# Q and K of groups two to five through DRAM by chunk, in one fixed order

## The chip, the cores and the metric

The kernel runs on one core of a Trainium2 chip. The metric is the device time of one execution in microseconds (us): TensorE (PE), VectorE (DVE), ScalarE (ACT), GpSimd (POOL) and SyncE (SP), which here only issues transfers, work side by side, and the time ends with the last of them.

## The reference

Two layers follow each other. The first is a gated linear recurrence over 768 steps, for 4 batches and 8 heads of width 48, with a complex gate a:

```python
scale = np.minimum(mag, 0.999) / (mag + 1e-06)
for t in range(S):
    new_re = ar * S_re - ai * S_im
    new_im = ar * S_im + ai * S_re
    S_re, S_im = (new_re + np.einsum('bhd,bhe->bhde', k[:, :, t], v[:, :, t]), new_im)
    y[:, :, t] = np.einsum('bhd,bhde->bhe', q[:, :, t], S_re)
```

The second takes y as 3072 rows x of 384 numbers through four experts of width 1024, weighted by the row's normalised probabilities p:

```python
for e in range(E):
    h = np.maximum(x @ w1[e], 0.0)
    out += p[:, e:e + 1] * (h @ w2[e])
```

## The kernel before

The 3072 steps are cut into 12 groups of 256 (G), numbered 0 to 11, three to a batch, and each group into two chunks of 128 (C). The recurrence is turned into matmuls: `norm` and `prefix` build the running products A of the gate, `finish` makes from them Q (q times A, in `head`) and K (k times the inverse of A, in `tail`, lines 435 to 443: five DVE instructions for the whole group, or five for each chunk). Both have the channels on the partitions, in rows of 128 steps; the matmuls want them by head, with the real part in partitions 0 to 47 and the imaginary part in 64 to 111. That turn is made by a trip through DRAM (`trip`, lines 447 to 459): two stores of a tile (real, imaginary), `q_d<-Q` or `k_d<-K` at line 451, and two loads back, `Qst<-q_d` or `Kst<-k_d` at line 456. All go through SP's queue, which takes them in order, each with a wait for what it needs. There is one buffer each of K, Qst and Kst, so a trip back can't begin before the last use of the group before.

For each chunk the attention then takes on PE: `turned` (K turned by the identity into KT, `ktp` L487), `increment` (`dp` L505, the chunk's addition to the state), `scores` (`sc` L517, Kst against Qst), and `values` (`yp` L531 from the state, L536 from the scores). `attention` (lines 606 to 624) does this for groups from 2 on, in three pieces, and the second chunk's scores stand in the second piece.

The MoE's first two experts run in the same stretch: while the attention of group g is made ready, the block of group g - 1 goes through 8 pairs of weight tiles, twice over 12 x 256 steps in all, with `ph` (L179, x times w1), `hh` and `hl` (the two parts of the ReLU's result, L188 on ACT and L189 on DVE) and `po` (L198, times w2); each expert's result is stored in DRAM (`acc_d`, from POOL's queue). From about 555 us on the other two experts run over blocks of 512 rows (L817, L830).

Several things set the order of the work. `moe1` calls `between(k)` ahead of each pair of weight tiles. There `advance` takes steps from the generator `stream`, which holds the vector work of the groups ahead, by a budget of STEP = 3.4 us a call, counted by estimates that the generator yields; and pieces of the attention are taken at k = first, first + 1 and first + 2. A scheduler then orders the instructions of each engine by its own estimate, where no dependence and no `behind` (an order without a semaphore) sets it. So the same Python order can come out in another order on an engine. In `front` (lines 664 to 719) the groups of HALF = (2, 3) make K by chunk and send each chunk of K alone, while Q goes as a whole; from group 4 on both go as a whole.

Of the kernel before, what the change touches and what calls it, by code (L numbers as in the profile page):

```python
# [57 lines left out]
NSEL = 2  # L58
XSEL = 3
FIRST = {1: 5, 2: 5, 3: 4, 4: 3}  # L60
STEP = 3.4
MORE = (1.9, 1.9, 0.5)
HALF = (2, 3)
HOFF = 96
WIDE = 32 + P + 48
DMA_SCRATCH = 4096
# [2 lines left out]
def fast_path(ctx, tc, qkP, aP, vP, probsP, w, out, flag):  # L69
# [159 lines left out]
    with ExitStack() as c1:  # L229
# [160 lines left out]
        def finish(g, A, qk):  # L390
            s = tmp(f"s2{g}")
            u = tmp(f"u2{g}")
            Q = big.tile([P, 2, NR, C + 1], F32, tag="tmp", name=f"Q{g}", bufs=TMP)
            K = big.tile([P, 2, NR, C], F32, tag="K", name=f"K{g}", bufs=1)

            def im(ap):
                return ap.rearrange("p (i m) -> p i m", i=SEG)

            def some(ap, lo, hi):
                if hi - lo == CG:  # L400
                    return ap.rearrange("p i m -> p (i m)")
# [12 lines left out]

            def head(lo, hi):
                nc.scalar.activation(some(a2a, lo, hi), some(A[:, 0], lo, hi), AF.Square)
                nc.scalar.activation(some(b2a, lo, hi), some(A[:, 1], lo, hi), AF.Square)
                for c in range(lo, hi):
                    a2, ic = some(a2a, c, c + 1), some(i0a, c, c + 1)
                    red = nc.vector.tensor_tensor_reduce(a2, a2, some(b2a, c, c + 1), scale=1.0, scalar=3e38,  # L420
                                                         op0=ALU.add, op1=ALU.min, accum_out=st_a2[:, c, g:g + 1])
                    nc.scalar.activation(ic, a2, AF.Ln, scale=2.0 ** A2_LOG[c], bias=a2b)
                    last_act = nc.scalar.activation(ic, ic, AF.Exp, scale=-1.0, bias=a2e[:, c:c + 1])
                for c in range(2):
                    ins = nc.vector.tensor_tensor(dst(Q[:, c, :, :C], lo, hi), rows(A[:, c], lo, hi),
                                                  rows(qk[:, 0], lo, hi), op=ALU.mult)
                    if g < NSEL and lo == 1:
                        behind(ins, red)
                if hi == CG:
                    nc.scalar.activation(Q[:, :, :, C].rearrange("p c (j n) -> p c j n", n=CG),  # L430
                                         A[:, :, SEG - 1, NS - 1::NS].unsqueeze(3).broadcast_to([P, 2, NJ, CG]),
                                         AF.Copy)
                return last_act

            def tail(lo, hi):
                a2, i0, t, kn = (some(x, lo, hi) for x in (a2a, i0a, ta, qk[:, 1]))
                nc.vector.tensor_tensor(t, a2, i0, op=ALU.mult)
                nc.vector.scalar_tensor_tensor(t, t, 2.0, i0, op0=ALU.subtract, op1=ALU.mult)
                nc.vector.tensor_tensor(t, kn, t, op=ALU.mult)
                for c in range(2):  # L440
                    last_dve = nc.vector.tensor_tensor(dst(K[:, c], lo, hi), rows(A[:, c], lo, hi), rows(ta, lo, hi),  # L441
                                                       op=ALU.mult)
                return last_dve

            return Q, K, head, tail

        def trip(nm, X, dst, lo=0, hi=CG):
            w = X.shape[-1] if hi == CG else C
            dt = dram.tile([2, HD, hi - lo, w], F32, name=nm)
            for c in range(2):  # L450
                nc.sync.dma_start(dt[c].rearrange("(j p) n t -> p j n t", p=P),
                                  X[:, c].rearrange("p (j n) t -> p j n t", n=CG)[:, :, lo:hi, :w])

            def back():
                for c in range(2):
                    landed = nc.sync.dma_start(dst[c * IM:c * IM + D, :, lo:hi, :w],
                                               dt[c].rearrange("(h d) n t -> d h n t", d=D))
                return landed
            return back

        def t_factors(g):
# [10 lines left out]
        def chunk(g, c, K, y):  # L472
# [8 lines left out]
            def turned():  # L481
                if last and g >= NSEL:
                    return
                for i in range(2):
                    kt_ps = ps_a.tile([P, HD], F32, tag="pa", name=f"ktp{g}_{c}_{i}")
                    for j in range(NJ):
                        ins = nc.tensor.transpose(kt_ps[:, j * P:(j + 1) * P], K[:, i, j * CG + c, :], ident)  # L487
                    nc.scalar.activation(KT[:, :, i * IM:i * IM + D],
                                         kt_ps.rearrange("p (h d) -> p h d", d=D), AF.Copy)
                return ins  # L490
# [173 lines left out]
        def front(g, A, qk):  # L664
# [34 lines left out]
            yield 3.9  # L699
            last["act"] = head(0, CG)  # L700
            yield 3.0
            qb = trip(f"q_d{g}", Q, Qst)
            if g in HALF:
                kb = []
                for c in range(CG):
                    last["dve"] = tail(c, c + 1)
                    yield 2.7
                    kb.append(trip(f"k_d{g}_{c}", K, Kst, c, c + 1))
                    if c == 0:
                        qb()  # L710
                for back in kb:
                    last["q"] = back()
            else:
                last["dve"] = tail(0, CG)
                yield 4.8
                kb = trip(f"k_d{g}", K, Kst)
                qb()
                last["q"] = kb()
            todo[g] = attention(g, (Q, K))
# [31 lines left out]
                        yield g, r  # L751

        work = stream()
        spent = {"g": 1, "us": 0.0}

        def advance(us, upto):
            spent["us"] -= us
            while spent["us"] < 0 and spent["g"] <= upto:
                r = next(work, None)
                if r is None:  # L760
                    spent["g"] = NG
                    return
                spent["g"], cost = r
                spent["us"] += cost

        nk = NF1 // 2
        for g in range(1, NG + 1):
# [3 lines left out]
            end = first + len(MORE) - 1  # L771

            def between(k, g=g, first=first, end=end):
                advance(STEP + (MORE[k - first] if first <= k <= end else 0.0), g + 1)
                if g == 1:
                    for i in range(NPRE + 2 * k, min(NPRE + 2 * k + 2, NF1)):
                        add_w(i, wts["hh"] if k else wts["x"])
                if g < NG and first <= k <= end:
# [2 lines left out]
                    r = next(todo[g], None)  # L781
                    if r is not None:
                        x[g] = split_x(g, r) if g < NSEL else r
                if k == max(end, nk - 1) and g in x and g >= NSEL:
                    x[g] = split_x(g, x[g])

            moe1(g - 1, *x.pop(g - 1), between)
            for k in range(nk, end + 1):
# [269 lines left out]
```

## Time and profile before

| | |
|---|---|
| median of 3 runs | 1018.09 us (1017.57 to 1020.13) |
| the profiled execution | 1015.63 us, its span 1013.9 us |
| mean granted clock of PE | 0.991 |
| busy: PE, DVE, ACT, POOL | 982.5, 591.2, 363.4, 34.4 us |
| PE busy, 0 to 110 us | 89.9 us |
| PE busy, 110 to 280 us (MoE blocks of groups 1 to 5 in the main) | 165.3 us |
| PE busy, 280 to 555 us | 275.0 us |
| PE busy, 555 to 1014 us | 452.3 us |

A row of a timeline is the start, the duration, the engine, the line, what it writes and reads, the shapes and how many in a row; in brackets stands the idle time of the engine ahead of it and what ended that. A row of waits has the total, the number and the longest. A row of the chain has start and duration of a piece of the chain of work that ended last. A matmul of two float32 operands counts twice, so that a chunk's eight scores are sixteen records. A stretch has its length, each engine's busy time (with instructions), PE's granted clock, the DMA engines' share and their GB/s.

### The profile page before, as it was taken

To read this page: it belongs to the slowest core of one execution; us is meant where nothing else is said; L and a number is where in the kernel's file an instruction comes from. 1 tells how busy PE (TensorE), PEld (TensorE's weight loads), DVE (VectorE), ACT (ScalarE), POOL (GpSimd) and SP (SyncE) were. 2 spreads that over 40 slices of the span, in tenths; PEclk is the share of its full clock that TensorE was granted. 3 is DMA by queue.
4 is the path that set the end of the run, shared out by engine and by line. 5 is a ranking of instruction groups with operands and counts; after the bars stand their busy time and mean duration, and the time that the engine had idled before them with its cause. 6 is when DMAs were issued, how large, how long until landed. Compare 5 with 4: busy or idle time off the path is not lost.

```text
span 1013.9 us, 16212 instructions
## 1 busy us (share of the span) xinstructions
PE 982.5 (97%) x6624; PEld 924.4 (91%) x6624; DVE 591.2 (58%) x1219; ACT 363.4 (36%) x653; POOL 34.4 (3%) x64
## 2 busy tenths in 40 slices
PE   4799999999999999999999999999999999999997
PEld 2699999999999999999999999989999999999996
DVE  6798988989797989888842363232232222321221
ACT  7746526436263553636332343121111211211110
POOL 5020000000000000000000000000000000000000
PEclk9899999999999999999999999999999999999999
DMA  9474356474554837457171691021030010100001
GB/s 318 148 147 150 82 154 155 154 184 125 149 164 119 213 99 196 129 145 198 54 164 33 232 334 41 1 88 38 1 125 1 32 63 1 63 1 1 32 1 35
DMA packets 78932, 110.78 MB, mean 109 GB/s; under 512 B 5440, under 2 KB 63344, under 8 KB 78848
## 3 DMA queue, kind: packets, MB, share of 16 engines
q1 hardware_dynamic: 74560, 94.53, 32.6%
q0 software_dynamic: 4288, 15.13, 5.0%
q8 instruction: 54, 0.88, 0.4%
q14 instruction: 30, 0.25, 0.1%
HBM read 73.71 MB, written 35.92 MB: 108 GB/s over the span
## 4 chain that ended last, share of the span: by engine, by line
PE 87%; DVE 4%; DMA 3%; ACT 2%; issue 1%; SPq 0%; DVEq 0%; ACTq 0%
PE pob L830 20%; PE phb L817 20%; PE ph L179 18%; PE po L198 17%; PE sc L517 5%; PE dp L505 2%; PE yp L536 2%; PE yp L531 2%; DMA Kst<-k_d 2%; PE ktp L487 1%; PE xp L567 1%; DMA k_d<-K 1%; DVE K L441 1%; PE qp L385 0%; DVE hl L189 0%
## 5 line engine op out<-in xcount | busy, mean ns | idle before, releaser
L823 DVE SCALAR_TENSOR_TENSOR hlb<-phb,hhb 128x512 fp32r<-128x512 f32 x96 | 66.4, 691 | 270.6 <-ACT hhb L822 270.6
L822 ACT ACTIVATE hhb<-phb 128x512 fp32r<-128x512 f32 x96 | 57.4, 598 | 314.6 <-PE phb L817 299.2
L830 PE MATMUL pob<-wlo,hhb 128*128 128x384 f32 x384 | 129.2, 337 | 0.0
L198 PE MATMUL po<-whi,hh 128*128 128x384 f32 x384 | 129.0, 338 | 0.0
L830 PE MATMUL pob<-whi,hhb 128*128 128x384 f32 x384 | 128.9, 336 | 0.0
L198 PE MATMUL po<-wlo,hh 128*128 128x384 f32 x384 | 128.8, 335 | 0.0
L198 PE MATMUL po<-whi,hl 128*128 128x384 f32 x384 | 124.4, 338 | 0.2 <-DVE hl L189 0.2
L830 PE MATMUL pob<-whi,hlb 128*128 128x384 f32 x384 | 120.4, 336 | 0.0
L188 ACT ACTIVATE hh<-ph 128x512 fp32r<-128x512 f32 x96 | 57.2, 596 | 158.3 <-PE ph L179 158.0
L179 PE MATMUL ph<-xha,whi 128*128 128x256 f32 x576 | 104.9, 287 | 0.8 <-ACT xha L166 0.8
L179 PE MATMUL ph<-xha,wlo 128*128 128x256 f32 x576 | 101.3, 283 | 0.0
L179 PE MATMUL ph<-xla,whi 128*128 128x256 f32 x576 | 101.0, 283 | 0.0
L189 DVE SCALAR_TENSOR_TENSOR hl<-ph,hh 128x512 fp32r<-128x512 f32 x96 | 66.1, 688 | 53.5 <-ACT hh L188 53.0
L817 PE MATMUL phb<-xhb,whi 128*128 128x512 f32 x288 | 91.8, 392 | 0.0
L179 PEld LDWEIGHTS ph<-xha,whi 128*128 128x128 f32 x576 | 86.1, 190 | 1.8 <-ACT xha L166 1.0
L179 PEld LDWEIGHTS ph<-xha,wlo 128*128 128x128 f32 x576 | 82.8, 190 | 0.5 <-issue 0.5
L179 PEld LDWEIGHTS ph<-xla,whi 128*128 128x128 f32 x576 | 82.8, 191 | 0.0
L817 PE MATMUL phb<-xlb,whi 128*128 128x512 f32 x288 | 82.7, 392 | 0.0
L817 PE MATMUL phb<-xhb,wlo 128*128 128x512 f32 x288 | 82.3, 393 | 0.0
L830 PEld LDWEIGHTS pob<-whi,hhb 128*128 128x128 f32 x384 | 72.1, 188 | 3.7
L830 PEld LDWEIGHTS pob<-wlo,hhb 128*128 128x128 f32 x384 | 72.1, 188 | 3.3
L198 PEld LDWEIGHTS po<-whi,hh 128*128 128x128 f32 x384 | 72.5, 189 | 0.5 <-issue 0.3
(165 smaller groups left out, 1574.8 us busy)
## 6 DMA issues: line engine op xcount, KB each, us to landing
wst<-w SPq DMA_DIRECT2D x25, 384.0 KB, 6.4
qk<-qkP SPq DMA_DIRECT2D x24, 384.0 KB, 6.5
acc_d<-acc POOLq DMA_DIRECT2D x24, 384.0 KB, 4.4
prev<-acc_d SPq DMA_DIRECT2D x24, 384.0 KB, 4.9
A<-aP SPq DMA_DIRECT2D x22, 384.0 KB, 7.9
q_d<-Q SPq DMA_DIRECT2D x20, 387.0 KB, 3.6
Qst<-q_d SPq DMA_DIRECT2D x20, 387.0 KB, 5.2
k_d<-K SPq DMA_DIRECT2D x16, 384.0 KB, 3.4
```

The source lines that it names most:

```text
L179: ins = nc.tensor.matmul(ph[:, u, :], wt[:, j * P:(j + 1) * P], xt[:, j, :], start=(n == 0), stop=(n == 3 * NJ - 1))
L188: wts["hh"] = nc.scalar.activation(hh, ph, AF.Relu)
L189: nc.vector.scalar_tensor_tensor(hl, ph, 0.0, hh, op0=ALU.max, op1=ALU.subtract)
L198: nc.tensor.matmul(po[t], ht[:, u, t * P:(t + 1) * P], wt[:, HD:], start=(i % FE == 0 and n == 0), stop=(i % FE == FE - 1 and n == 2))
L505: nc.tensor.matmul(d_ps[:, h, :], KT[:, h, :], vc[:, h * D:(h + 1) * D], start=True, stop=True)
L517: nc.tensor.matmul(s_ps[:, h, :], Kc[:, hf * 4 + h, :], Qc[:, hf * 4 + h, :], start=True, stop=True)
L531: ins = nc.tensor.matmul(yo, st[:, o:o + n], Qc[:, o // D, :], start=True, stop=False)
L536: ins = nc.tensor.matmul(yo, vc[:, o:o + n], sc[h // 4][:, h % 4, :], start=first, stop=True)
L817: nc.tensor.matmul(ph, wt[:, j * P:(j + 1) * P], xt[:, j, :], start=(n == 0), stop=(n == 3 * NJ - 1))
L822: nc.scalar.activation(hh, ph, AF.Relu)
L823: nc.vector.scalar_tensor_tensor(hl, ph, 0.0, hh, op0=ALU.max, op1=ALU.subtract)
L830: ins = nc.tensor.matmul(po[t], ht[:, t * P:(t + 1) * P], wt[:, HD:], start=(i % FE == 0 and n == 0), stop=(i % FE == FE - 1 and n == 2))
```

## The change

- HALF now holds groups 2 to 5. There K is made and sent by chunk, and so is Q: each chunk of Q has its own DRAM tile, its own two stores and two loads.
- One order of issue is set in SP's queue with `behind`: the stores of both chunks of Q, the return of Q's first chunk, the stores of K's first and of K's second chunk, the return of K's first chunk, of Q's second, of K's second. Before, the scheduler placed these by its estimate.
- `front` yields None between head and tail. `advance` then holds the stream until the attention of the group before has been emitted (`over`). K's buffer is taken when the tail begins, not with Q's.
- `between` takes the piece of the attention first and advances the stream after it; before it was the other way round. STEP becomes an empty table that gives 3.4 for every group, as before.

From group 6 on the trips go as a whole, as before, though hold and later `advance` act there too. Groups 0 and 1 go another way (`near_attention`).

```diff
-STEP = 3.4
+STEP = {}
-HALF = (2, 3)
+HALF = (2, 3, 4, 5)
...
-            K = big.tile([P, 2, NR, C], F32, tag="K", name=f"K{g}", bufs=1)
+            K = []
...
             def tail(lo, hi):
+                if not K:
+                    K.append(big.tile([P, 2, NR, C], F32, tag="K", name=f"K{g}", bufs=1))
...
-        def trip(nm, X, dst, lo=0, hi=CG):
+        def trip(nm, X, dst, lo=0, hi=CG, prev=None):
...
-                nc.sync.dma_start(dt[c].rearrange("(j p) n t -> p j n t", p=P),
+                sent = nc.sync.dma_start(dt[c].rearrange("(j p) n t -> p j n t", p=P),
...
+                if prev is not None:
+                    behind(sent, prev)
...
-            qb = trip(f"q_d{g}", Q, Qst)
             if g in HALF:
+                qb = [trip(f"q_d{g}_{c}", Q, Qst, c, c + 1) for c in range(CG)]
+                yield None
+                landed = qb[0](qb[1].sent)
                 kb = []
                 for c in range(CG):
                     last["dve"] = tail(c, c + 1)
                     yield 2.7
-                    kb.append(trip(f"k_d{g}_{c}", K, Kst, c, c + 1))
-                    if c == 0:
-                        qb()
-                for back in kb:
-                    last["q"] = back()
+                    kb.append(trip(f"k_d{g}_{c}", K[0], Kst, c, c + 1, landed if c == 0 else kb[0].sent))
+                landed = kb[0](kb[1].sent)
+                landed = qb[1](landed)
+                last["q"] = kb[1](landed)
             else:
+                qb = trip(f"q_d{g}", Q, Qst)
+                yield None
...
+        spent = {"g": 1, "us": 0.0, "hold": 0}
+        over = {0}
...
             while spent["us"] < 0 and spent["g"] <= upto:
+                if spent["hold"] not in over:
+                    spent["us"] = 0.0
+                    return
...
-                spent["us"] += cost
+                if cost is None:
+                    spent["hold"] = spent["g"] - 1
+                else:
+                    spent["us"] += cost
...
-                advance(STEP + (MORE[k - first] if first <= k <= end else 0.0), g + 1)
...
+                    if k == end:
+                        over.add(g)
                 if k == max(end, nk - 1) and g in x and g >= NSEL:
                     x[g] = split_x(g, x[g])
+                advance(STEP.get(g, 3.4) + (MORE[k - first] if first <= k <= end else 0.0), g + 1)
```

More of the change, by code (lines that the diff above doesn't have):

```diff
@@ L440, in tail @@
                 for c in range(2):
-                    last_dve = nc.vector.tensor_tensor(dst(K[:, c], lo, hi), rows(A[:, c], lo, hi), rows(ta, lo, hi),
+                    last_dve = nc.vector.tensor_tensor(dst(K[0][:, c], lo, hi), rows(A[:, c], lo, hi), rows(ta, lo, hi),
                                                        op=ALU.mult)
@@ L450, in trip, with back @@
             for c in range(2):
-                nc.sync.dma_start(dt[c].rearrange("(j p) n t -> p j n t", p=P),
-                                  X[:, c].rearrange("p (j n) t -> p j n t", n=CG)[:, :, lo:hi, :w])
-            def back():
+                sent = nc.sync.dma_start(dt[c].rearrange("(j p) n t -> p j n t", p=P),
+                                         X[:, c].rearrange("p (j n) t -> p j n t", n=CG)[:, :, lo:hi, :w])
+                if prev is not None:
+                    behind(sent, prev)
+            def back(prev=None):
                 for c in range(2):
@@ L457, in back @@
                                                dt[c].rearrange("(h d) n t -> d h n t", d=D))
+                    if prev is not None:
+                        behind(landed, prev)
                 return landed
+            back.sent = sent
             return back
@@ L486, in turned @@
                     for j in range(NJ):
-                        ins = nc.tensor.transpose(kt_ps[:, j * P:(j + 1) * P], K[:, i, j * CG + c, :], ident)
+                        ins = nc.tensor.transpose(kt_ps[:, j * P:(j + 1) * P], K[0][:, i, j * CG + c, :], ident)
                     nc.scalar.activation(KT[:, :, i * IM:i * IM + D],
@@ L707, in front @@
                     yield 2.7
-                    kb.append(trip(f"k_d{g}_{c}", K, Kst, c, c + 1))
-                    if c == 0:
-                        qb()
-                for back in kb:
-                    last["q"] = back()
-            else:
+                    kb.append(trip(f"k_d{g}_{c}", K[0], Kst, c, c + 1, landed if c == 0 else kb[0].sent))
+                landed = kb[0](kb[1].sent)
+                landed = qb[1](landed)
+                last["q"] = kb[1](landed)
+            else:
+                qb = trip(f"q_d{g}", Q, Qst)
+                yield None
                 last["dve"] = tail(0, CG)
                 yield 4.8
-                kb = trip(f"k_d{g}", K, Kst)
+                kb = trip(f"k_d{g}", K[0], Kst)
                 qb()
@@ L753, in fast_path @@
         work = stream()
-        spent = {"g": 1, "us": 0.0}
+        spent = {"g": 1, "us": 0.0, "hold": 0}
+        over = {0}
         def advance(us, upto):
```

## The prediction

> **What bounds the kernel now.** I read the page first, then who waited for whom on PE, PE's timeline at the waits, the busy time of short stretches, the chain of waits, and the transfers.
>
> ```profile
> PE 982.5 (97%) x6624; PEld 924.4 (91%) x6624; DVE 591.2 (58%) x1219; ACT 363.4 (36%) x653; POOL 34.4 (3%) x64
> PE lp L147 <- DMA wst<-w: 9.6, 1, 9.6
> PE qp L385 <- DVE Q L425: 6.3, 1, 6.3
> PE sc L517 <- DMA Kst<-k_d: 3.8, 3, 1.8
> PE po L198 <- DVE hl L189: 0.2, 1, 0.2
> ```
>
> PE is busy for 982.5 of 1013.9 us, and the change takes no matmul away, so only PE's idle time, or matmuls that run slowly, can be won. Of the waits the first two lie in the start, which the change does not touch. The one it touches is the third: scores (sc) three times wait for K's way back from DRAM, 3.8 us in all. The other half of the loss shows where those waits end:
>
> ```profile
> 136.00 2.05 PE L517 MATMUL sc<-Qst,Kst 112*128 112x128 f32 x16 [1.03 <-DMA Kst<-k_d]
> 137.99 0.43 PE L531 MATMUL yp<-Qst,G 112*64 112x128 f32 x4
> ...
> 220.84 1.38 PE L517 MATMUL sc<-Qst,Kst 112*128 112x128 f32 x5 [1.84 <-DMA Kst<-k_d]
> ...
> 220.84 3.65 PE sc L517 x16
> ...
> 268.28 3.47 PE L517 MATMUL sc<-Qst,Kst 112*128 112x128 f32 x16 [0.93 <-DMA Kst<-k_d]
> 271.67 0.60 PE L531 MATMUL yp<-Qst,G 112*48 112x128 f32 x4
> ```
>
> The waits are those of groups 2, 4 and 5 (1.03, 1.84, 0.93 us). The same sixteen score records take 2.05 us after the first, but 3.65 and 3.47 us after the others (the row without a shape is the chain's). The granted clock says why:
>
> ```profile
> 132.12:135.54 3.42, 2.86 (x25) 2.73 (x23) 2.40 (x7) 0.00 (x0) 0.00 (x0) 1.00 0.83 213
> 217.45:220.87 3.42, 1.58 (x18) 1.48 (x16) 1.96 (x5) 0.60 (x1) 0.00 (x0) 1.00 1.10 204
> 265.25:268.66 3.41, 2.48 (x24) 2.35 (x23) 2.44 (x7) 0.00 (x0) 0.00 (x0) 1.00 1.07 253
> 220.80:224.60 3.80, 3.76 (x18) 3.79 (x19) 1.10 (x4) 0.00 (x0) 0.00 (x0) 0.55 0.82 316
> 268.00:272.00 4.00, 3.72 (x20) 3.42 (x20) 1.65 (x5) 0.00 (x0) 0.00 (x0) 0.58 0.69 267
> ```
>
> The second column is PE's busy time, the third from the end the clock. 0.55 over 3.8 us is about 3.4 us at half speed. The stretches before had PE busy for 1.58 and 2.48 of 3.4 us; the one with 2.86 (group 2) was not followed by half speed. So a wait of about a microsecond here also costs the slow matmuls behind it: 3.65 - 2.05 = 1.60 us in group 4; in group 5 3.47 - 2.05 = 1.42 and 0.60 - 0.43 = 0.17 for the next four, 1.59. Waits and slow stretches together are 3.80 + 3.19 = 7.0 us, the most that this change can win.
>
> **The change part by part.** The chain of waits shows the way that is to be shortened, in groups 4 and 5 (start, length). Behind it stand the half-size transfers of group 3, which goes by chunk already (two issues on SP's queue, then us from issue to landing), and the two sizes of K's products (mean ns behind the comma):
>
> ```profile
> 210.85 3.83 DMA k_d<-K
> ...
> 214.70 6.00 DMA Kst<-k_d
> ...
> 255.53 1.83 DVE K L441 x2
> ...
> 257.37 2.86 DMA k_d<-K
> ...
> 260.29 7.94 DMA Kst<-k_d
> 166.31 0.91 SPq L451 DMA_DIRECT2D k_d<-K  x2
> k_d<-K SPq DMA_DIRECT2D x4, 192.0 KB, 4.2
> 171.03 0.84 SPq L456 DMA_DIRECT2D Kst<-k_d  x2
> DMA to landing us min/median/max: 3.2/3.5/3.7
> L441 DVE TENSOR_TENSOR K<-A,u 128x384 f32<-128x384 f32 x8 | 4.1, 551 | 0.0
> L441 DVE TENSOR_TENSOR K<-A,u 128x768 f32<-128x768 f32 x4 | 3.6, 951 | 0.0
> ```
>
> *Products by chunk (groups 4, 5).* Five instructions of 951 ns become ten of 551 (other tail lines have the same two sizes), 0.75 us more DVE work a group. This is what DVE does in group 4, after (u holds the steps of the tail, K its product; hl is the MoE's, G the state, L338 the next group's norm):
>
> ```order
> L439 TENSOR_TENSOR u_2091<-s_2090,u_2091 128x24x16
> L564 TENSOR_TENSOR G_1_2264<-G_1_2264,TA 112x384
> L440 SCALAR_TENSOR_TENSOR u_2091<-u_2091 128x24x16
> L189 SCALAR_TENSOR_TENSOR hl_0_2412<-ph_0_2392,hh_0_2411 128x512
> L441 TENSOR_TENSOR u_2091<-qk_2084,u_2091 128x24x16
> L338 TENSOR_TENSOR u_2535<-s_2534,u_2535 128x768
> L443 TENSOR_TENSOR K_2441<-A_1594,u_2091 128x8x3x16 x2
> L189 SCALAR_TENSOR_TENSOR hl_1_2467<-ph_1_2447,hh_1_2466 128x512
> ```
>
> Rows that read alike are left out. Both chunks' first three steps stand ahead of the first K, so the first chunk needs eight half instructions, 8 x 0.55 = 4.4 us, against 5 x 0.95 = 4.75: it is ready some 0.4 us sooner only. The added DVE work hides beside PE, which waits 0.2 us for hl in all; without that cover it is 1.5 us. PE and ACT run the same instructions as before. The hold and the later call of the stream only move them: the tail comes after the last piece of the attention before, where the buffer of K comes free anyway, so I cost them at nothing beyond the places shown here; if they delayed K's products, group 4 would show it first.
>
> *Transfers by chunk, first chunks first.* SP's queue for group 4, before:
>
> ```order
> L478 DMA v_1_2517<-vP 128x384
> L451 DMA q_d_2494<-Q_2187 128x3x258 x2
> L456 DMA Qst<-q_d_2494 48x8x258 x2
> L451 DMA k_d_2502<-K_2188 128x3x256 x2
> L456 DMA Kst<-k_d_2502 48x8x256 x2
> L280 DMA qk_2676<-qkP 128x768 x2
> ```
>
> and after:
>
> ```order
> L485 DMA v_1_2542<-vP 128x384
> L453 DMA q_d_0_2433<-Q_2092 128x3x128
> L453 DMA q_d_1_2436<-Q_2092 128x3x129
> L460 DMA Qst<-q_d_0_2433 48x8x128 x2
> L453 DMA k_d_0_2482<-K_2441 128x3x128 x2
> L453 DMA k_d_1_2525<-K_2441 128x3x128 x2
> L460 DMA Kst<-k_d_0_2482 48x8x128 x2
> L460 DMA Qst<-q_d_1_2436 48x8x129 x2
> L460 DMA Kst<-k_d_1_2525 48x8x128 x2
> L280 DMA qk_2660<-qkP 128x768 x2
> ```
>
> Before the first chunk's return now stands only what it needs and the second chunk's store, with Q's second half behind it. The first K back waits in SP's queue for the second chunk's products; those come at most 2.5 us after the first chunk's (two K of 551 ns and an L341 of 951 ns with one hl, by its size between them), less than the 2.9 to 4.2 us that a store takes to land, so this wait is hidden; uncovered, it costs what the products come late, and behind it queue the rest and the next loads of qk and A, which are wanted a group later. Four groups issue 24 more transfers, on a queue that stands idle for most of a group.
>
> Now each wait. *Group 4*: PE was ready at 220.84 - 1.84 = 219.0. The whole K came back at 214.70 + 6.00 = 220.7, 9.9 us after its products, which ended as the store was issued, at 210.8. The first half: 0.5 to the second issue, 3.8 for the store (group 4's own), 0.5 again, 3.5 for the way back (group 3's) = 8.3, from 210.4: 218.7. That is even, since two ph less now stand ahead of the scores. With the 2.9 of group 5's store 1 us is to spare; with 4.2, and the 4.4 of group 2 below, it is 220.0, a wait of 1.0. I take 0.2.
>
> *Group 5*: the scores move forward. PE before and after:
>
> ```order
> L179 MATMUL ph_2_3051<-xla_2853,whi_557 128x256 x3
> L198 MATMUL po_0_0_2943<-whi_524,hh_1_2975 128x384
> ...
> L198 MATMUL po_0_1_2944<-whi_535,hl_1_2976 128x384
> L179 MATMUL ph_3_3146<-xha_2852,whi_568 128x256 x3
> L505 MATMUL dp_0_3026<-v_0_3012,KT 112x48 x8
> L517 MATMUL sc_0_0_3037<-Qst,Kst 128x128 x4
> ```
>
> and after (ph is the first MoE product, po the second, dp the state's increment):
>
> ```order
> L179 MATMUL ph_2_3113<-xha_2889,wlo_558 128x256 x3
> L512 MATMUL dp_0_3066<-v_0_3052,KT 112x48 x8
> L524 MATMUL sc_0_0_3077<-Qst,Kst 128x128 x4
> L524 MATMUL sc_0_1_3084<-Qst,Kst 128x128 x4
> L179 MATMUL ph_2_3113<-xla_2890,whi_557 128x256 x3
> L198 MATMUL po_0_0_2992<-whi_524,hh_1_3021 128x384
> ```
>
> Twelve po and six ph now come behind the scores instead of ahead of them.
>
> ```profile
> 250.01 2.08 PE po L198 x12
> 252.10 2.16 PE ph L179 x18
> 254.92 0.69 DVE L189 SCALAR_TENSOR_TENSOR hl<-ph,hh 128x512 fp32r<-128x512 f32 x1
> acc_d<-acc POOLq DMA_DIRECT2D x1, 384.0 KB, 5.5
> ```
>
> They are 2.08 + 0.72 = 2.8 us, so PE asks at 267.35 - 2.8 = 264.5. The first K products now stand ahead of the hl at 254.92 instead of behind it, so they end near 254.9. From there 0.5 + 2.9 + 0.5, and back: here the store of acc_d (5.5 us) ran beside K's 7.94; with half the bytes (group 4's 6.0 against group 3's 3.5 says 2.5 us less) 5.4. That is 264.2, just in time; 3.5 leaves 2 us, and 7.9 a wait of 2.2. I take 0.2.
>
> *Group 2*, by chunk already (with the landing of its first two returns):
>
> ```profile
> DMA to landing us min/median/max: 3.5/4.0/4.4
> 129.86 0.32 SPq L456 DMA_DIRECT2D Kst<-k_d  x1
> 130.27 2.09 SPq L451 DMA_DIRECT2D k_d<-K  x2
> 132.42 3.35 SPq L456 DMA_DIRECT2D Kst<-k_d  x3
> ```
>
> The return that PE waited for was issued at 132.42, behind the second chunk's store, which held the queue for 2.09 us. Now that store goes first and both returns follow at about 129.9 and 130.4; at 4.4 us they land by 134.8, and PE was ready at 134.97. I take 0, with 0.2 left over for later groups. Sum: 7.0 - 0.6 = 6.4 us less.
>
> The Trainium skill (TensorE: Matmul & The Clock Gate, "HAM oscillation — how this bites in real kernels") states that the clock falls back only after PE is idle for some 3.4 us. The trace disagrees: half speed follows idle times of 1.84 and 0.93 us; by the rule this change would win 3.8 - 0.6 = 3.2 us.
>
> The profiled execution took 1015.63 us, the runs 1018.09 (1017.57 to 1020.13). Minus 6.4 that is 1009.2 by the first and 1011.7 by the second. No row says what the 2.5 us are; if the runs had a third half-speed stretch (1.6 us, behind group 2's wait), it goes too. I take 0.7 of it: **1011.0 us**.
>
> **The rivals.**
> 1. *Half speed stays.* If the low clock does not come from these waits, only 3.2 us go: 1018.09 - 3.2 = 1014.9, on the edge between faster and no change. Against it: both half-speed stretches stand right behind a wait, and after the stretch of group 2 in which PE was busy for 2.86 of 3.4 us there is none. This is what the skill's rule named above comes to. Chance 0.08.
> 2. *One wait stays.* Groups 4 and 5 come out within a few tenths. At the dear end above, group 4 keeps 1.0 and its slow stretch of 1.6 where 0.2 was taken: 1011.0 + 2.4 = 1013.4. Chance 0.14.
> 3. *The wait moves on.* Group 6 stays whole:
>
> ```profile
> 301.57 1.33 SPq L456 DMA_DIRECT2D Kst<-k_d  x2
> DMA to landing us min/median/max: 4.5/5.2/5.8
> 309.53 2.02 PE L517 MATMUL sc<-Qst,Kst 112*128 112x128 f32 x16
> 110.00:280.00 170.00, 165.25 (x1312) 159.81 (x1313) 147.09 (x325) 78.68 (x145) 3.25 (x6) 0.98 0.56 147
> ```
>
> Its K lands near 302.6 + 5.8 = 308.4, 1.1 us before the scores. PE comes 6 us sooner, and DVE, busy for 147 of 170 us here, has 0.75 us a group more; if groups 6 and 7 then wait 1.2 us each with slow stretches, 2 x 2.8 = 5.6 come back: 1016.6, no change. For it: the small slack; against it: products of a group follow PE's earlier work and move with it. Chance 0.12.
> 4. *The second chunk comes late* (slower). Its K is now the last of six returns. Chunk 1's scores in group 4 begin at 226.89 on this trace's timeline:
>
> ```profile
> 226.89 0.38 PE L517 MATMUL sc<-Qst,Kst 112*128 112x128 f32 x1
> ```
>
> 6.05 us after chunk 0's, 4.45 without the slow stretch. Four returns behind the first pair come in time at group 3's pace (issued 0.45 us apart and landing 3.2 and 3.7 us after issue, so 0.95 us each: 3.8); at the 2.5 us that 192 KB cost between groups 3 and 4 they need 10.0, a wait of 5.5 in groups 4 and 5 with 1.6 behind each: 14.2, 1025.2 us. It decides from about 2 us for each return. Chance 0.06.
>
> That the order is not as told can be left out: the queue's rows show it.
>
> **How the numbers follow.** A measurement here tells 0.3% (3 us) from no change. Forecast 0.60 (its own range 1008.0 to 1013). Faster: 0.60 + 0.14 and half of rival 1's 0.08 = 0.78; same 0.12 + 0.04 = 0.16; slower 0.06. The range goes from 1008.0 (1015.63 - 7.0, less the 0.5 by which the lowest run lies under the median) to 1015.7, past rivals 1 and 2 by that spread; rivals 3 and 4, 0.18, are left out.
>
> **What would show it.** Right: no PE wait for Kst in groups 2 to 5 over 0.3 us, score records of 2.05 us there, clock 1.00 from 40 to 1000 us. Wrong: slow score records without a wait ahead (rival 1), sc waits at group 4 or 5 (2), at group 6 or 7 (3), or on a second chunk (4); waits for hl above 1 us would mean that DVE is the bound.

## The result, and the profile after

The changed kernel took 1013.04 us in the median of 7 runs (1011.32 to 1016.55), the kernel before 1018.25 us in runs beside it: a ratio of 0.9941 (95% interval 0.9922 to 0.9960); the medians lie 5.2 us apart. The forecast was 1011.0 us (1008.0 to 1015.7). Two later measurements of the same kernel (experiments 6 and 12) gave 0.9985 (0.9970 to 0.9999) and 0.9964 (0.9947 to 0.9980). All three intervals lie below 1, that of experiment 6 only just, so the change wins something; how much is not sure, between 1 and 6 us. It depends on two things that the prediction did not know of: where PE's instruction fetches fall, and where the windows of the clock begin.

The profiled execution took 1012.58 us, 3.1 us less than that of before (1015.63). The page of the kernel after, busy times:

```profile
PE 978.7 (97%) x6624; PEld 921.1 (91%) x6624; DVE 590.7 (58%) x1229; ACT 362.7 (36%) x653; POOL 34.2 (3%) x64
```

And who PE waited for there (total, times, longest):

```profile
PE sc L524 <- issue: 4.3, 3, 1.9
```

The scores still wait, for 4.3 us in three places; before it was 3.8. "issue" only says that the page found no releaser; the times below show that it is K's way back. What got less is PE's busy time, 982.5 to 978.7 us, with the same 6624 records. The first scores of groups 2, 4, 5 and 6 on PE's timeline:

```profile
136.65 2.02 PE L524 MATMUL sc<-Qst,Kst 112*128 112x128 f32 x16 [1.94 <-issue]
...
219.19 2.02 PE L524 MATMUL sc<-Qst,Kst 112*128 112x128 f32 x16
...
263.13 2.02 PE L524 MATMUL sc<-Qst,Kst 112*128 112x128 f32 x16 [1.69 <-issue]
...
306.41 2.02 PE L524 MATMUL sc<-Qst,Kst 112*128 112x128 f32 x16 [0.63 <-issue]
```

Group 4's wait of 1.84 us is gone. Group 2's grew from 1.03 to 1.94 us, group 5's from 0.93 to 1.69, and group 6 has a new one of 0.63. Yet all the scores run at full speed: 2.02 us each time. The profile records the granted clock in windows of 3.413 us. Stretches cut along this grid (PE's busy time is the second column, its clock the third from the end):

```profile
135.27:138.68 3.41, 2.04 (x18) 1.95 (x20) 1.34 (x5) 0.00 (x0) 0.00 (x0) 1.00 1.22 181
138.68:142.09 3.41, 3.41 (x33) 2.99 (x35) 2.44 (x8) 0.60 (x1) 0.00 (x0) 1.00 1.03 363
261.56:264.97 3.41, 1.83 (x17) 1.87 (x17) 1.61 (x4) 0.00 (x0) 0.00 (x0) 1.00 1.26 167
264.97:268.38 3.41, 3.41 (x25) 2.85 (x25) 3.34 (x11) 0.60 (x1) 0.00 (x0) 1.00 1.04 304
```

PE was busy for only 1.83 of 3.41 us in one of them, less than in the 2.48 that half speed followed in the kernel before; here none followed. So in the profiled execution the two half-speed stretches (3.2 us) went, and the waits, which were to take them along, stayed.

What SP's queue did for group 4:

```profile
210.26 3.31 SPq L453 DMA_DIRECT2D k_d<-K  x4
214.21 0.92 SPq L460 DMA_DIRECT2D Kst<-k_d  x2
215.18 0.98 SPq L460 DMA_DIRECT2D Qst<-q_d  x2
216.20 0.98 SPq L460 DMA_DIRECT2D Kst<-k_d  x2
```

How long K's four returns took from issue to landing, in groups 2, 4 and 5:

```profile
DMA to landing us min/median/max: 5.6/7.0/7.5
...
DMA to landing us min/median/max: 3.1/4.5/6.0
...
DMA to landing us min/median/max: 6.3/6.7/8.1
```

The order is as told, and group 4's first chunk was back in 3.1 and 3.5 us. In groups 2 and 5 the same two transfers took 5.6 to 6.9 us. The trace counts each landing in sixteen parts, as many as the core has DMA engines, and the transfer has landed with the last of them. The table has, in us, when the first of the two returns of a group's first scores was issued, the last two parts of the second return (for groups that go whole, too), when PE had nothing left but the scores ("asked"), and a fetch begun while they were under way, which is explained below:

```
kernel, group   first return issued   15th part   16th part   PE asked   fetch (length)
after, 2        129.08                134.58      136.56      134.71     130.54 (1.81)
after, 4        214.21                218.26      218.33      219.19     none
after, 5        255.56                261.54      263.05      261.45     258.44 (0.88)
after, 6        299.18                306.03      306.32      305.78     none
before, 2       129.86                135.76      135.96      134.98     130.45 (1.46)
before, 4       213.74                220.69      220.70      219.00     none
before, 5       259.12                267.52      268.23      267.34     260.57 (1.23)
```

In groups 2 and 5 of the kernel after, fifteen parts are back when PE asks, or within 0.1 us of it. The sixteenth is 1.98 and 1.51 us late. The page's row on queue 8 shows what may have held that one part:

```profile
q8 instruction: 54, 0.88, 0.4%
```

The same row for 129 to 135 us:

```profile
q8 instruction: 1, 0.02, 1.9%
```

Queue 8 brings instructions: 54 transfers of 16 KB, each a single packet, one for about every 245 of the 13,248 records of PE and PEld. 1.9% of sixteen engines over 6 us is 1.8 us on one. The reading is that the engine which carried this packet brought its share of K's return later than the others, and K landed with it. The trace does not name a packet's engine, so this stands on the experiments. The length of the packet does not give the delay: in group 2 1.81 us stand beside 1.98, but in group 5 0.88 beside 1.51. What adds the rest is open. The Trainium skill (Runtime: NRT & Kernel Launch, "Instruction fetch mechanics") describes these refills of 16 KB, which the trace agrees with, and calls their cost mostly hidden. Here the two late parts together are about 3.5 us of PE's time.

### The profile page after: what moved, and what is told of

The parts are those of the page before. It is cut to its first block, busy times and chain, and to the rows that moved or that the text cites. A ratio compares the mean times of both kernels' runs of the same rounds, so it can differ in the third digit from the quotient of the medians.

```text
span 1010.8 us, 16259 instructions
## 1 busy us (share of the span) xinstructions
PE 978.7 (97%) x6624; PEld 921.1 (91%) x6624; DVE 590.7 (58%) x1229; ACT 362.7 (36%) x653; POOL 34.2 (3%) x64
## 4 chain that ended last, share of the span: by engine, by line
PE 91%; DMA 2%; DVE 2%; ACT 2%; POOL 1%; issue 1%; SPq 0%; DVEq 0%; POOLq 0%
PE pob L849 20%; PE phb L836 20%; PE ph L179 19%; PE po L198 18%; PE sc L524 4%; PE dp L512 2%; PE yp L543 2%; PE yp L538 2%; PE ktp L494 1%; PE xp L574 1%; DMA Kst<-k_d 1%; DMA mask_d<-mask 1%; PE qp L385 0%; DMA q_d<-Q 0%; DMA maskp<-mask_d 0%
```

## The experiments

**Theory A**: the waits that are left come from the one late engine, so they follow the place of the fetches. **Theory B**: they come from the stores and loads that share the engines with K's return. For the clock: a wait of about a microsecond is followed by half speed wherever it lies (C), or only in the second half of a grid window (D).

**1. Fetches moved by 27 tiny matmuls at the start.**

```diff
+HOFF = 96; NSPARE = 27
...
+        A, spare = [load_a(0, halves)], ps_a.tile([M, 8], F32, tag="pa", name="spare")
+        wst = {i: stage1(i, PRE) for i in range(NST)}; [nc.tensor.matmul(spare, ident[:, 0:M], ident[:, 0:8], start=True, stop=True) for _ in range(NSPARE)]
```

> The kernel after, with 27 tiny float32 matmuls more at the very start, where TensorE has nothing to do; no transfer of groups 2 to 7 stands in another place. They shift only when TensorE's instructions are fetched (16 KB for every 256 instructions, on queue 8), by 108 instructions, some 7 us earlier at group 2. Theory A (late engine): the waits of 1.94 us in group 2 and 1.69 us in group 5 come from one DMA engine of sixteen that such a fetch holds up while K's first chunk comes back (fetches at 130.5 and 258.4 us). Then the fetches fall near 123 and 251 us, the last of the sixteen parts comes within 0.3 us of the fifteenth in groups 2 and 5, and the waits there fall to 0.3 us or less; the fetches now fall near 303 and 348 us, so group 6's wait grows from 0.63 to 1.2 to 2 us and group 7 gets one of 0.3 to 1 us. Waits in all 4.3 to about 2.5, time 1 to 2 us under the kernel after. Theory B (shared transfers): the waits come from the stores and loads that run beside K's return; nothing there is changed, so 1.9 and 1.7 us stay in groups 2 and 5, and group 6 keeps 0.6.

Measured: 1017.31 us, ratio 0.9988 (0.9972 to 1.0004). First scores of groups 2, 5 and 7:

```profile
141.94 2.02 PE L524 MATMUL sc<-Qst,Kst 112*128 112x128 f32 x16
...
266.69 2.02 PE L524 MATMUL sc<-Qst,Kst 112*128 112x128 f32 x16
...
356.82 1.35 PE L524 MATMUL sc<-Qst,Kst 112*128 112x128 f32 x10 [1.16 <-issue]
```

The waits of groups 2 and 5 are gone, and group 7, where the next fetch fell (353.1 us), has one: its sixteenth part came 1.26 us after the fifteenth. That is A. Three points missed: group 6 waited only 0.14 us (a fetch at 302.5, sixteenth part 0.19 us behind: the engine caught up); the waits in all were 1.3 us where 2.5 were expected; and the time did not fall, since the added matmuls made the scheduler order the start otherwise: group 2's scores come 5.3 us later than in the kernel after.

**2. The same with 15.** The edit is that above with 15 for 27.

> The same with 15 tiny matmuls, 60 instructions, some 4 us earlier. Theory A (late engine): fetches near 127, 254.5, 306 and 351 us. The one near 127 meets the store of K's first chunk in group 2 and not its return, so group 2 waits between 0 and 1 us; group 5 waits 0.3 us or less, group 6 0.3 to 0.9 us, group 7 nothing: 1 to 2 us in all instead of 4.3, and the time falls 2.5 to 3.5 us, to about 1010 us. Theory B (shared transfers): 4.3 us of waits and the time of the kernel after, 1013 us.

Measured: 1010.20 us, 0.9926 (0.9901 to 0.9951). No wait for K over 0.2 us in groups 2 to 7; fetches at 127.2 and 251.2 us. A holds, B does not: no transfer of these groups was given another place in its queue. (The start is in another order here too; experiment 5 takes that away.)

**3. Groups 4 and 5 whole again.**

```diff
-HALF = (2, 3, 4, 5)
+HALF = (2, 3)
```

> The kernel after with HALF = (2, 3): groups 4 and 5 go whole through DRAM again, the order of issue, the hold and the later call of the stream stay. If the smaller transfers of groups 4 and 5 carry the gain, their waits come back as before (1.8 and 0.9 us), with or without slow matmuls behind, and the time is 1016 to 1018.5 us. If the gain lies in the hold and in the order alone, it stays at 1013 us.

Measured: 1016.36 us, 0.9983 (0.9966 to 0.9999). Groups 4 and 5:

```profile
221.48 2.82 PE L524 MATMUL sc<-Qst,Kst 112*128 112x128 f32 x16 [2.87 <-DMA Kst<-k_d]
...
269.19 2.79 PE L524 MATMUL sc<-Qst,Kst 112*128 112x128 f32 x16 [1.25 <-DMA Kst<-k_d]
```

Both groups wait, each with half speed behind. Group 4's wait is back, so the smaller transfers have a share in what ended it. Not all of the 2.87 us is theirs: a fetch at 209.1 us made the last parts of K's stores 1.58 and 1.43 us late. For group 5 this run says nothing, since it waits in the kernel after too (1.69 us), and a fetch lies in both. Nor does the time show what the smaller transfers are worth: 0.9983 is also what the kernel after came to in experiment 6 (0.9985), and the waits add up to nearly the same, 4.1 us here and 4.3 there.

**4. Eighty waits in the last stage.**

```diff
+HOLD = (256, 512, 768, 1024, 1280, 1536)
...
+            if r > 0:
+                w = HOLD[(5 * i + 7 * r) % len(HOLD)]
+                mark = nc.tensor.matmul(ph[:, 0:8], ident, gate[:, 0:8], start=True, stop=True)
+                for ins in order["po"]:
+                    behind(mark, ins)
+                nc.vector.scalar_tensor_tensor(gate[:, :w], gate[:, :w], ph[:, 0:1], gate[:, :w], op0=ALU.mult, op1=ALU.mult)
+                nc.tensor.matmul(ph[:, 0:8], ident, gate[:, 0:8], start=True, stop=True)
...
```

> The kernel after, in whose last stage TensorE is made to wait 80 times: ahead of each first product from the second block of 512 rows on, a tiny matmul, a VectorE instruction of 256 to 1536 elements on its result, and a tiny matmul on that one's. Nothing is left out. The waits are 0.6 to 2.1 us, at all places of the 3.41 us grid on which the clock records begin. Theory C (length): a wait of about a microsecond (0.93 us or more) is followed by 3.41 us at half clock wherever it lies; that gives 50 half-speed records or more. Theory D (place): half speed follows only where the idle time falls in the second half of a grid window, 0.85 us or more of its last 1.7 us; that gives 15 to 30 records, none for waits in the first half of a window. The Trainium skill (TensorE: Matmul & The Clock Gate) has the clock fall after some 3.4 us of idle time; by that rule there is no record at all.

The waits, as the profile sums them up:

```profile
PE phb L845 <- DVE gate L844: 118.3, 80, 3.8
```

Eighteen half-speed records in the last stage (one of them two windows long; the one at the very end is left aside): C (50 or more) and the Trainium skill's rule (none) both fall. D has the right number and the wrong places: a wait of 1.70 us that ended 1.2 us ahead of its window's end was followed by half speed, one that held the last 1.67 us of a window was not. By idle time alone, all fourteen windows with 1.78 us of it or more were followed by half speed, four of the eleven with 1.57 to 1.76 us, and none below. That leaves open the half speed behind a wait of 0.93 us in the kernel before, and its absence behind 1.57 us of idle time in a window of the kernel after. There the products differ: 48 columns of a moving operand in some, 384 in others. The columns that went through PE in each window order all of these cases, if a float32 column is counted 1.75 times, a weight fitted to them: half speed follows a window with fewer than about 3,000 (2,966 at most with it here, 3,124 at least without). So a theory E (idle time) and a theory F (columns) went on.

**5. The shift without a new order at the start.**

```diff
+HOFF = 96; NSPARE = 15
...
+        A = [load_a(0, halves)]; spare = ps_a.tile([1, 1], F32, tag="pa", name="spare"); [nc.tensor.matmul(spare, ident[:, 0:1], ident[:, 0:1], start=True, stop=True) for _ in range(NSPARE)]
```

> As with 15 tiny matmuls before, but of one row and column each, so that no other instruction of any engine changes its place (before, the start came out in another order and lost about 2 us). Theory A (late engine): waits for K's first chunk of 0.3 us or less in each of groups 2 to 7, the sixteenth part of each return within 0.5 us of the fifteenth; no start of another order, so 0.5 to 2 us under the first version: 1008 to 1010 us. Theory B (shared transfers): 4.3 us of waits, 1013 us.

Measured: 1008.96 us, 0.9929 (0.9910 to 0.9948), all six runs between 1007.67 and 1009.92. Groups 2, 4, 5 and 6:

```profile
136.12 2.02 PE L524 MATMUL sc<-Qst,Kst 112*128 112x128 f32 x16
...
218.68 2.02 PE L524 MATMUL sc<-Qst,Kst 112*128 112x128 f32 x16
...
260.97 2.02 PE L524 MATMUL sc<-Qst,Kst 112*128 112x128 f32 x16
...
303.66 2.02 PE L524 MATMUL sc<-Qst,Kst 112*128 112x128 f32 x16
```

The only row of waits for the scores, beside that of the first groups:

```profile
PE sc L524 <- DVE pf L354: 0.2, 1, 0.2
```

4.3 us of waits have become 0.2. Apart from the added products every engine runs the same instructions in the same order as in the kernel after, by their names and shapes in the two traces. This is the profile that the prediction described. The other order of the start in experiment 2 cost nothing that the ratios show (0.9926 there, on another chip).

**6. The kernel after once more, on the same chip as 5 and 7.**

> The kernel after once more, beside the others on the same chip: 1012 to 1014 us. Theory A (late engine): the same fetches in groups 2 and 5 (130.5 and 258.4 us, within 0.5), the same waits there of 1.5 to 2 us.

Measured: 1014.48 us beside 1015.69 of the kernel before, 0.9985 (0.9970 to 0.9999), a little above the 1012 to 1014 us expected. Groups 2, 5 and 6, then the windows ahead of and behind the first two:

```profile
136.26 2.05 PE L524 MATMUL sc<-Qst,Kst 112*128 112x128 f32 x14 [1.68 <-issue]
...
264.59 3.76 PE L524 MATMUL sc<-Qst,Kst 112*128 112x128 f32 x16 [2.03 <-issue]
...
311.03 1.24 PE L524 MATMUL sc<-Qst,Kst 112*128 112x128 f32 x9 [0.88 <-issue]
```

```profile
134.25:137.67 3.42, 1.74 (x16) 1.64 (x16) 1.35 (x5) 0.00 (x0) 0.00 (x0) 1.00 1.24 186
137.67:141.08 3.41, 3.41 (x18) 2.86 (x17) 2.93 (x8) 0.00 (x0) 0.00 (x0) 0.50 1.02 338
260.55:263.96 3.41, 2.00 (x21) 1.88 (x19) 2.10 (x6) 0.00 (x0) 0.00 (x0) 1.00 1.24 160
263.96:270.79 6.83, 6.20 (x26) 6.23 (x27) 3.23 (x9) 0.60 (x1) 0.00 (x0) 0.50 1.11 271
```

The same waits, the sixteenth part 2.05 and 2.00 us late, and here half speed does follow, three windows of it. The waits fall elsewhere on the grid, which begins at another point in each execution: group 2's lies whole in one window, where the first profile had it split 0.56 and 1.38 us between two. The mean granted clock of the runs, 0.994 in the first measurement and 0.992 here (0.992 for the kernel before beside it), says that this is about half of why one kernel came to 0.9941 and to 0.9985: 0.0024 of the clock is 2.4 us, and the ratios lie 4.5 us apart. The rest is open. (The fetches were at 130.9 and 259.9 us; the second was 1.5 us off its first place, not the 0.5 expected.)

**7. The kernel before with its fetches moved** (25 of the one-column matmuls, nothing else).

> The kernel before with 25 tiny matmuls at the start and nothing else, which put the fetches of TensorE's instructions some 6 us earlier, off K's returns in groups 2, 4 and 5. If the fetches alone made the waits of the kernel before, they go and the time falls to 1012 to 1014 us. If they carry only what the sixteen parts show (0.7 us of group 5's wait, 0.2 of group 2's), group 5 waits 0.2 to 0.4 us, group 4 still 1.8, group 2 still 0.8 to 1, and the time is 1015.5 to 1017.5 us.

Measured: 1010.89 us, 0.9957 (0.9943 to 0.9972); groups 2, 4 and 5:

```profile
135.58 2.05 PE L517 MATMUL sc<-Qst,Kst 112*128 112x128 f32 x16 [0.68 <-DMA Kst<-k_d]
...
219.43 1.80 PE L517 MATMUL sc<-Qst,Kst 112*128 112x128 f32 x14 [0.85 <-DMA Kst<-k_d]
...
264.31 1.94 PE L517 MATMUL sc<-Qst,Kst 112*128 112x128 f32 x15
```

More than either case allowed, again with every engine's order unchanged. Group 4's wait fell from 1.84 to 0.85 us: in the kernel before a fetch at 209.86 had made the last parts of K's two stores 0.75 and 0.62 us late, and the returns wait for the stores. (In the kernel after a fetch at 210.04 made K's first two stores 0.99 and 0.91 us late, and K was still back 0.86 us before PE asked: there K by chunk has the slack to bear it.) Group 5's wait fell from 0.93 to 0.03 us though its transfers still go whole, so it was the fetch's and not the size's. And no half speed followed in the profiled execution. Moving the fetches is worth 4.8 us by itself on this chip; with it, the change is worth another 1.9 us (1010.89 to 1008.96).

**8. Narrower products, the same waits.** Each first product of the last stage of experiment 4 is issued as two of 256 columns.

```diff
-                    nc.tensor.matmul(ph, wt[:, j * P:(j + 1) * P], xt[:, j, :],
...
+            for hs in (slice(0, G), slice(G, T2)):
...
+                        ins = nc.tensor.matmul(ph[:, hs], wt[:, j * P:(j + 1) * P], xt[:, j, hs],
```

> As the kernel with 80 waits in the last stage (which gave 16 records of half speed there), but its first products are issued as two of 256 columns each in the place of one of 512: the same work and the same waits, TensorE as busy as before, yet with some 290 ns for 256 columns in the place of 392 for 512. Theory E (idle time): half speed follows a 3.41 us window in which TensorE stood idle for 1.6 us or more; then there are again 15 to 25 records. Theory F (columns): it follows a window in which fewer than some 3,000 columns of the moving operand went through TensorE (a float32 column counting 1.5 to 1.75 times); then a wait of 0.6 us is enough at most places and there are 50 records or more.

Seventeen records (the expectation gives experiment 4 sixteen; its trace has eighteen). My expectation for F was wrong, and so E is not yet told from F. The span is 1210.6 us, against 1208.4 in experiment 4: two products of 256 columns take as long as one of 512. The 290 ns was how long one is under way, not the time to the next (in experiment 9 that is 120 ns at 256 columns and 231 ns at 512).

**9. Very narrow products, no waits.**

```diff
+            w = (T2, 32, 64, 128, 256, T2)[r]
+            for t in range(0, T2, w):
...
+                        ins = nc.tensor.matmul(ph[:, t:t + w], wt[:, j * P:(j + 1) * P], xt[:, j, t:t + w],
```

> The kernel after; in the last stage the first products of a block of 512 rows are issued in pieces of 32 columns (second block of rows), 64 (third), 128 (fourth), 256 (fifth) and 512 (first and last). Same work and results, nothing waits more than before. Theory E (idle time): half speed needs a 3.41 us window with 1.6 us or more of idle TensorE; there is none in the last stage, so no half-speed record there before the end. Theory F (columns): it needs a window in which fewer than some 3,000 columns went through TensorE. At some 60 ns for a narrow product a window of 32-column pieces holds 1,800 columns, one of 64-column pieces 3,600 or fewer: half speed in 20 windows or more of the second block though TensorE is busy all the time, few or none in the third, none from the fourth on.

Stretches in the block with 32 columns, with 64, and with 256 and 512:

```profile
839.00:938.00 99.00, 99.00 (x450) 99.00 (x449) 2.07 (x3) 1.79 (x3) 0.00 (x0) 0.50 0.00 1
1225.00:1430.00 205.00, 205.00 (x1088) 205.00 (x1087) 11.38 (x17) 7.76 (x13) 0.00 (x0) 0.62 0.00 1
1560.00:1670.00 110.00, 110.00 (x649) 103.94 (x648) 24.50 (x38) 15.59 (x26) 0.00 (x0) 1.00 0.02 8
```

The page's clock over the span, in 40 slices:

```profile
PEclk9999999999999999555555555555655666999999
```

PE is busy for 99.00 of 99.00 us, at half clock throughout. E falls: idle time is not what it takes. In these blocks 26 windows without any idle time were followed by half speed, with 960 to 2,736 columns in each; the emptiest that was not had 3,099. F stands, with a size that I had wrong, the 60 ns: at full clock the products follow each other after 111 to 112 ns, whether they have 32, 64 or 128 columns. That makes some 980, 1,970 and 3,940 columns a window, so the block with 64 is at half clock for most of its length too, and the one with 128 is not.

**10. Q's second chunk back ahead of K's first** (on the kernel of experiment 5, groups 2 to 5).

```diff
-                landed = kb[0](kb[1].sent)
-                landed = qb[1](landed)
+                landed = qb[1](kb[1].sent)
+                landed = kb[0](landed)
```

> The kernel with 15 one-column matmuls at the start (1008.96 us, no wait for K), with one thing of the change's order undone in groups 2 to 5: the two returns of Q's second chunk stand ahead of those of K's first chunk. If the order of the returns matters as the prediction has it (each return of 96 KB in the queue takes about 1 us), K's first chunk lands 1.9 to 2.4 us later; the slack of 0.1, 3.6, 1.1 and 0.1 us in groups 2 to 5 leaves waits of about 2, 0, 1 and 2 us, and the time is 1012.5 to 1017 us. If the first chunks are early enough in any order, it stays within 1 us of 1009.

Measured: 1014.77 us beside 1019.23 of the kernel before, 0.9955 (0.9941 to 0.9968), where experiment 5 had 0.9929 on another chip. Groups 2, 4 and 5:

```profile
137.85 2.02 PE L524 MATMUL sc<-Qst,Kst 112*128 112x128 f32 x16 [1.01 <-DMA Kst<-k_d]
...
222.25 3.06 PE L524 MATMUL sc<-Qst,Kst 112*128 112x128 f32 x14 [1.33 <-DMA Kst<-k_d]
...
269.26 1.91 PE L524 MATMUL sc<-Qst,Kst 112*128 112x128 f32 x15 [1.16 <-DMA Kst<-k_d]
```

3.5 us of waits instead of 0.2. The order among the returns matters as told, at half the price in groups 2 and 5: there the scheduler also put MoE products (1.4 and 2.2 us of them) between the state's increments and the scores, so PE asked later.

**11. K by chunk without the order** (the kernel before, 25 one-column matmuls, HALF = (2, 3, 4, 5)).

> The kernel before with the same 25 tiny matmuls (1010.89 us; waits of 0.68, 0.85 and 0.03 us in groups 2, 4 and 5) and HALF = (2, 3, 4, 5): K by chunk in groups 4 and 5 too, Q whole, no order set, no hold. If K by chunk is what ends group 4's wait, 0.7 us of waits are left (group 2's) and the time is 1009.5 to 1010.5 us. If the set order is needed for that, group 4 keeps 0.5 us or more (as group 2 does, whose second chunk's stores stand ahead of a return) and the time stays at 1010.5 to 1011.5 us.

Measured: 1011.07 us beside 1019.23, 0.9921 (0.9907 to 0.9935). Groups 2, 4 and 5:

```profile
137.03 3.35 PE L517 MATMUL sc<-Qst,Kst 112*128 112x128 f32 x14 [1.52 <-DMA Kst<-k_d]
...
221.14 2.02 PE L517 MATMUL sc<-Qst,Kst 112*128 112x128 f32 x16
...
263.23 2.02 PE L517 MATMUL sc<-Qst,Kst 112*128 112x128 f32 x16
```

K by chunk alone ends the wait of group 4 (group 5's was gone in experiment 7 already), and in both it leaves more slack than the change (K's first chunk is there 1.5 and 3.6 us ahead, since its return need not stand behind the second chunk's stores). The set order is needed in group 2 only, where the wait grew from experiment 7's 0.68 to 1.52 us, with half speed behind it. The time lies in the range that I gave the other case (1010.5 to 1011.5), but on another chip, where the kernel before takes 1019.23 us; by the ratio this kernel is no worse than experiment 5's 0.9929. So with the fetches out of the way no measurement here shows that the set order, the hold and Q by chunk win time beyond K by chunk.

**12. The kernel after a third time.**

> The kernel after a third time: its two measurements so far (0.9941 and 0.9985 of the kernel before) differ by more than their intervals. Theory A (late engine) has the same fetches meet K's returns of groups 2 and 5 each time, so 4 to 5 us of waits again, of which as many are followed by half speed as the 3.41 us grid happens to allow: a ratio between 0.993 and 0.999, and runs that lie 1.7 us apart by the number of half-speed records. If the second measurement was the odd one, the ratio is 0.993 to 0.995 and the granted clock 0.994 or more in most runs.

Measured: 1014.66 us beside 1018.50, 0.9964 (0.9947 to 0.9980). Half of what I expected was wrong. The fetch of group 2 came at 133.4 us this time, 3 us later, and held nothing up; the waits of groups 2 and 5 were 0.37 and 0.90 us. Group 6 waited instead:

```profile
305.92 3.75 PE L524 MATMUL sc<-Qst,Kst 112*128 112x128 f32 x16 [2.73 <-issue]
```

Here all sixteen parts were late (the fifteenth at 305.65, PE asked at 303.19), with no fetch near. The larger part of the delay lay ahead of the returns: K's first store, beside Q's second return, took 5.59 us, where it took 3.30 in experiment 5 and 2.82 in the kernel before. Then K's second return, with the store of acc_d issued between the two, took 6.99 us against 5.93 in experiment 5. So for group 6, which still goes whole, theory B fits; no run changed those transfers to test it.

## Why the prediction was right, and where not

The time lay in the range, at the upper end of what the forecast claimed as its own (1008.0 to 1013), and the working was right in part. By its own signs it failed: waits for K in groups 2, 5 and 6. That the first measurement came so near the forecast is in part luck: with the same waits, but more half speed behind them, the same kernel was only 1.2 us under the kernel before in experiment 6.

- **Group 4**: right. Its first chunk was forecast back at 218.7 and landed at 218.33; PE was forecast to ask at 219.0 and asked at 219.19.
- **Group 5**: the sum of its chain was right, relative to PE. It came out 3 us earlier as a whole (PE asked at 261.45 instead of 264.5), because what group 4 saved moves both K's products and PE. "Just in time" was what fifteen of the sixteen parts were, 0.1 us behind PE. But the wait that smaller transfers were to end there was the fetch's: in experiment 7 it went with the transfers whole.
- **Group 2**: forecast 134.8 against 134.97; fifteen parts at 134.58 against 134.71. Right but for the sixteenth.
- **The residual of 0.6 us** is the term that failed: 4.3 us of waits were left. It priced a return by the landing times of other groups, as if all that varies were the bytes beside it. That one part of sixteen may come up to 2 us late beside an instruction fetch of 0.9 to 2.2 us was in none of the rows that I quoted, though group 5's 7.94 us held 0.7 us of it. With the fetches out of the way (experiment 5) 0.2 us are left.
- **The half-speed term** (3.19 us) came out in the first profile by luck, its reason being wrong: "a wait of about a microsecond here also costs the slow matmuls behind it". Waits of 1.94 and 1.69 us did not, in experiment 6 those of 1.68 and 2.03 us did. What counts is the columns in a window of a grid that lies otherwise in each execution.
- **The rivals**: the first, half speed that stays though the waits go, was seen nowhere (experiment 5 has neither). The second had nearly the measured time (1013.4), with its waits in groups 2 and 5 and not 4. The third, the wait that moves on to group 6, took place in each profile of the kernel after: 0.63, 0.88 and 2.73 us, and in experiments 4, 8 and 9, which change the last stage alone: 1.23, 1.13 and 2.93. I gave it 0.12. The fourth did not come: the last of the six returns landed 1.1 us ahead of its use in group 4 and 0.16 us ahead in group 5, closer than I thought.
- **The sum** of 6.4 us is about what the change gives where no fetch meets K (experiment 5: 1015.69 to 1008.96 us, 6.7 us). But 4.8 us are what the kernel before gains by moved fetches alone, which leaves 1.9 us for the change. Of the prediction's two halves, waits and clock, neither was the change's alone.

## What to carry to other kernels

A transfer lands with the slowest of its sixteen parts, so look at the parts, not only at the landing, before you blame its size or its neighbours. A wait with little slack can be made or ended by where PE's instruction fetches fall, and these move with every instruction added ahead: compare two orders of a kernel with the fetches in mind, in several executions, or give the transfer 2 us of slack. And when half-speed stretches come and go between executions, the mean granted clock of each run says how much of a difference is theirs.

## What the runs showed of the hardware

**One late part.** Groups 2 to 11 of fourteen profiles have 140 first returns of K; of each I took the one of the pair that landed last. In 42 a fetch of queue 8 began between the first issue and 1 us ahead of the fifteenth part; there the sixteenth came 0.82 us behind it in the median and 2.05 us at most. In the other 98 it was 0.07 us in the median and 0.54 at most. The delay does not follow the fetch's length (correlation -0.03 over the 42), but when it began: it was over 1.04 us only where the fetch began 2 to 4.5 us ahead of the fifteenth part; with more time than that it was 1.04 us or less, so the late part catches up.

**Half speed by columns.** Over the same profiles some 3,960 grid windows of 3.413 us were at full clock from 45 us on; 73 were followed by half speed, the one at each span's end left aside. I laid out each record's columns from its start at 1.4 a nanosecond, an assumed rate. Of some 2,600 windows with only the MoE's products, 62 were followed by it; the fullest of these had about 2,970 columns, and the emptiest of the others about 2,985. With other rates of layout some windows within 150 columns of 3,000 change sides. Windows with float32 products fit the same bound if such a column counts 1.75 times; that weight is fitted, not measured apart. A typical window has about 7,450. The windows that the text spoke of:

```
kernel, window from   columns   next window
before, 217.5         1255      half
before, 265.2         2933      half
after, 135.3          3976      full
after, 261.6          3666      full
experiment 6, 134.3   2784      half
experiment 6, 260.6   2117      half
experiment 12, 301.9  1040      half
```

The Trainium skill (TensorE: Matmul & The Clock Gate, Part 1) has a free-running window of 3413 ns, and the records agree. That it takes an idle window to fall back, as the Trainium skill has it there, does not hold here.
